# Scores of the first 256 tokens: plain float32 products instead of split ones, with the split of their keys done later

## The chip, the cores and the metric

The kernel runs on one core of a Trainium2 chip. The metric is the device time of one execution in microseconds; the figure given for a kernel is the median of several executions. TensorE (PE) multiplies, VectorE (DVE) and ScalarE (ACT) do elementwise work, GpSimd (POOL) and SyncE (SP) here mostly set up constants and issue transfers.

## The reference

A block-causal attention, a square-relu MLP and a top-1 mixture of experts, in float32:

```python
B, H, S, D = 4, 8, 576, 64
scores = (1/sqrt(D)) * q @ k.T          # block-causal mask, blocks of 64
scores = where(block_i >= block_j, scores, -1e9)
attn = softmax(scores, denominator + 1e-9) @ v
x = attn as [B*S, H*D]                  # 2304 x 512
x = relu(x @ w_in)**2 @ w_out           # 512 -> 2048 -> 512
e = argmax(x @ w_gate + bias[modality]) # 8 experts, 512 -> 1024 -> 512
out = gate * relu(x @ w1[e]) @ w2[e]
```

## The kernel before, in words

The attention is cut into units: for each batch five groups of query rows (`CHUNKS`: four of 128 rows and one of 64), and in each group four pairs of heads. One unit is `attn_pair`, which calls `attn_scores` (scores, softmax, transposes) and `attn_values` (the product with v, and the copy into the x block that the MLP reads). The MLP works on nine blocks of 256 tokens; block j is a list of 16 units and a last step, and `interleave` (L845) puts the attention units that later blocks need between the MLP units of a block. The first eight attention units (batch 0, query groups 1 and 2, so tokens 0 to 255) have nothing to stand beside; they come before the first MLP block. The order on each engine is then made by a planner (`schedule_with_timeline_sim`, L1004) from its own estimates; an instruction traced inside `tc.issue_after(x)` stays behind x on x's engine.

Products that need float32 accuracy are made in one of two ways. Either both operands are split into a high part (a cast to fp32r) and a low part (a subtract), and fp32r products of the parts are added; or both are plain f32. The first MLP block uses plain f32 (`ffn_units32`, L537), all others and the attention use split operands. The inputs q and k are stored twice along the 128 partitions (64 head dimensions each). `split_k` (L225) casts a key tile on ACT (L234) and overwrites the lower 64 partitions with the low part on DVE (L235); `attn_scores` (L281) scales the queries by 0.125 while it casts them on ACT (L300) and gets the low part on DVE (L301). Two fp32r products (L312, L313) per head then give the scores, `both` (L304) handles the two heads of a unit at once: mask, maximum (L315), exp (L317), sum, reciprocal (L320), normalise (L272), transposes (L327), copy (L264).

For batch 0 the keys come in two parts: the first 256 columns (`kpre2`, tiles kw[0] and kw[1]) and the other 320 (`kpre`, kw[2] to kw[4]). Before, part 0 is split just ahead of each of the first four units, part 1 ahead of the four units of query group 3, there inside `issue_after` of the last x copy (L412) of the first eight units. The kw tiles, early v, early q and the MLP's raw weights share one ring of 33 slots, tag `w` (L139), and raw weights are joined from their 64-bit form by `join_weight64` (L150: one ACT and three DVE steps, L156 to L161). PSUM has one bank for the MLP's hidden product (`BANKS`, L46: "h" 1) and two for scores.

Of the kernel before, what the change touches and what calls it, by code (L numbers as in the profile page):

```python
# [20 lines left out]
P = 128  # L21
# [31 lines left out]
def tile_attention_mlp_moe(ctx: ExitStack, tc: tile.TileContext, qT2, kT2, v, w_in, w_out,  # L53
# [168 lines left out]
        kraw[b, h] = apool.tile([P, S], F32, tag="p", bufs=6, name="kraw")  # L222
        nc.sync.dma_start(kraw[b, h], kT2[b, h])

    def split_k(b, hp, part=None):  # L225

        heads = (2 * hp, 2 * hp + 1)
        if part != 1:
            ks2 = apool.tile([P, 2, S], F32R, tag="ks", bufs=4, name=f"ks{b}_{hp}")
            for j, h in enumerate(heads):  # L230
                kst[b, h] = ks2[:, j]

        def split(ks, raw):
            nc.scalar.copy(ks, raw)  # L234
            nc.vector.tensor_sub(ks[HD:P], raw[HD:P], ks[HD:P].bitcast(F32))  # L235

        if part == 0:
            split(ks2[:, :, 0:KS], kpre2[hp])
        else:
            for h in heads:  # L240
                if part is None:
                    split(kst[b, h], kraw[b, h])
                else:
                    split(kst[b, h][:, KS:S], kpre[h])

    def load_v(b, hp, nk):
        vt = apool.tile([P, 5, P], F32, tag="v", bufs=2, name="v")
# [33 lines left out]
    def attn_scores(b, r0, nr, hp, pt2=None):  # L281

        nk = r0 + nr
        nkb = (nk + P - 1) // P
        if (b, r0) in qst:
            qraw = qst[b, r0][:, 2 * hp:2 * hp + 2]
        else:
            qraw = apool.tile([P, 2, P], F32, tag="qraw", bufs=2, name="qraw")
            nc.sync.dma_start(qraw[:, :, :nr], qT2[b, 2 * hp:2 * hp + 2, :, r0:r0 + nr].rearrange("h d s -> d h s"))
        vt = vpre[hp] if b == 0 and nk <= 512 else load_v(b, hp, nk)  # L290
        qlo = apool.tile([P, 2 * P], F32R, tag="qlo", bufs=2, name="qlo")
        qhi = apool.tile([P, 2 * P], F32R, tag="qhi", bufs=2, name="qhi")
        if nr == P:
            dh, dl = (z.rearrange("p (j c) -> p j c", j=2) for z in (qhi, qlo))
        else:

            dh, dl = (z.rearrange("p (j c) -> p j c", j=4)[:, 0::3] for z in (qhi, qlo))
            for z in (qhi, qlo):
                nc.gpsimd.memset(z[:, HD:3 * HD].bitcast(F32), 0.0)
        nc.scalar.mul(dh, qraw[:, :, :nr], 0.125)  # L300
        nc.vector.scalar_tensor_tensor(out=dl, in0=qraw[:, :, :nr], scalar=0.125, in1=dh.bitcast(F32),  # L301
                                       op0=ALU.mult, op1=ALU.subtract)

        def both():  # L304

            nmx = apool.tile([P, 3], F32, tag="nmx", bufs=4, name="nmx")
            sm = apool.tile([P, 4], F32, tag="sm", bufs=4, name="sm")
            pb = apool.tile([P, S], F32, tag="p", bufs=6, name="p")[:, 0:512].rearrange("p (j c) -> p j c", j=2)
            sb = pbank("s", 2).rearrange("p (j c) -> p j c", j=2)
            for j in range(2):  # L310
                ks = kst[b, 2 * hp + j]
                nc.tensor.matmul(sb[:, j], qhi[:, j * P:(j + 1) * P], ks[:, 0:256], start=True, stop=False)  # L312
                nc.tensor.matmul(sb[:, j], qlo[:, j * P:(j + 1) * P], ks[:, 0:256], start=False, stop=True)  # L313
            nc.vector.memset(sb[0:64, :, nk - 64:nk], NEG)
            nc.vector.tensor_reduce(out=nmx[:, 0:2], in_=sb[:, :, :nk], axis=AX.X, op=ALU.max, negate=True)  # L315
            for j in range(2):
                nc.scalar.activation(out=pb[:, j, :nk], in_=sb[:, j, :nk], func=AF.Exp, bias=nmx[:, j:j + 1],  # L317
                                     accum_out=sm[:, j:j + 1])
            nc.vector.tensor_scalar_add(sm[:, 0:2], sm[:, 0:2], 1e-9)
            nc.vector.reciprocal(sm[:, 2:4], sm[:, 0:2])  # L320
            for j in range(2):
                normalise(pb[:, j, :nk], sm[:, 2 + j:3 + j])
            pt = apool.tile([P, 5, P], F32, tag="pt", bufs=2, name="pt")
            tv = pbank("pt", 1).rearrange("p (k q) -> p k q", q=P)
            for i in range(2 * nkb):
                kb = i % nkb
                nc.tensor.transpose(tv[:, i], pb[:, i // nkb, kb * P:(kb + 1) * P], ident)  # L327
            evac_copy(pt[:, 0:2 * nkb], tv[:, 0:2 * nkb])
            return [pt, pt[:, nkb:2 * nkb]]

        def finish_rows(pb, nmx, sm, banks, parts, pt=None):

            npt = len(parts)
            for i, (c0, nv) in enumerate(parts):
                nc.vector.tensor_reduce(out=nmx[:, i:i + 1], in_=banks[i][:, :nv], axis=AX.X, op=ALU.max,  # L335
                                        negate=True)
            if npt == 2:
                nc.vector.tensor_tensor(nmx[:, 0:1], nmx[:, 0:1], nmx[:, 1:2], op=ALU.min)
            for i, (c0, nv) in enumerate(parts):
                nc.scalar.activation(out=pb[:, c0:c0 + nv], in_=banks[i][:, :nv], func=AF.Exp,  # L340
                                     bias=nmx[:, 0:1], accum_out=sm[:, i:i + 1])
            if npt == 2:
                nc.vector.scalar_tensor_tensor(out=sm[:, 0:1], in0=sm[:, 0:1], scalar=1e-9, in1=sm[:, 1:2],
                                               op0=ALU.add, op1=ALU.add)
            else:
                nc.vector.tensor_scalar_add(sm[:, 0:1], sm[:, 0:1], 1e-9)
            nc.vector.reciprocal(sm[:, 2:3], sm[:, 0:1])
            normalise(pb[:, :nk], sm[:, 2:3])
            if pt is None:
                pt = apool.tile([P, 5, P], F32, tag="pt", bufs=2, name="pt")  # L350
            for g0 in range(0, nkb, 4):
                kbs = list(range(g0, min(g0 + 4, nkb)))
                tv = pbank("pt", 1).rearrange("p (k q) -> p k q", q=P)
                for kb in kbs:
                    k0 = min(kb * P, nk - P)
                    nc.tensor.transpose(tv[:, kb - g0], pb[:, k0:k0 + P], ident)
                evac_copy(pt[:, kbs[0]:kbs[-1] + 1], tv[:, 0:len(kbs)])
            return pt

        def single(j):  # L360
            ks = kst[b, 2 * hp + j]
            nmx = apool.tile([P, 3], F32, tag="nmx", bufs=4, name="nmx")
            sm = apool.tile([P, 3], F32, tag="sm", bufs=4, name="sm")
            pb = apool.tile([P, S], F32, tag="p", bufs=6, name="p")[:, 0:512]
            sb = pbank("s", 2)
            nc.tensor.matmul(sb[:, :nk], qhi[:, j * P:(j + 1) * P], ks[:, :nk], start=True, stop=False)
            nc.tensor.matmul(sb[:, :nk], qlo[:, j * P:(j + 1) * P], ks[:, :nk], start=False, stop=True)
            nc.vector.memset(sb[0:64, nk - 64:nk], NEG)
            return finish_rows(pb, nmx, sm, [sb], [(0, nk)], None if pt2 is None else pt2[:, 4 * j:4 * j + nkb])

        def tail():

            half = nk // 2
            nmx = apool.tile([P, 3], F32, tag="nmx", bufs=4, name="nmx")
            sm = apool.tile([P, 3], F32, tag="sm", bufs=4, name="sm")
            pb = apool.tile([P, S], F32, tag="p", bufs=6, name="p")
            banks = []
            for c0 in (0, half):
                sb = pbank("s", 2)
                for j in range(2):  # L380
                    ks = kst[b, 2 * hp + j]
                    for z in (qhi, qlo):
                        nc.tensor.matmul(sb[:, :half], z[:, j * P:(j + 1) * P], ks[:, c0:c0 + half],
                                         start=(j == 0 and z is qhi), stop=(j == 1 and z is qlo))
                banks.append(sb)
            pt = finish_rows(pb, nmx, sm, banks, [(0, half), (half, half)])
            return [pt[:, :, 0:HD], pt[:, :, HD:P]]

        pts = tail() if nr < P else both() if nk <= 256 else [single(j) for j in range(2)]
        return pts, vt  # L390

    def attn_values(b, r0, nr, hp, pairs):
# [45 lines left out]
    def attn_units():  # L438

        res = []  # L440
        for b in range(B):
            for ci, (r0, nr) in enumerate(CHUNKS):
                for hp in range(H // 2):
                    def f(b=b, ci=ci, r0=r0, nr=nr, hp=hp):
                        if b == 0 and ci == 0:
                            split_k(b, hp, 0)
                        elif b == 0 and ci == 2:
                            with tc.issue_after(x_end[0].ins):
                                split_k(b, hp, 1)
                        elif b and ci == 0:  # L450
                            split_k(b, hp)
                        attn_pair(b, r0, nr, hp)
# [555 lines left out]
```

## Time and profile before

| | us |
|---|---|
| median of 3 executions | 878.53 |
| lowest and highest | 877.90, 879.07 |
| the profiled execution, whole | 882.9 |
| its span, first to last instruction | 881.1 |

PE is busy for 97% of the span, PE's weight loads for 83%, DVE for 57%, ACT for 45%, POOL for 8%. The first of 40 slices of the span has PE at 5 tenths, the second at 7, then 9 or more nearly throughout; the DMA engines are full in the first two slices (311 and 353 GB/s). In the profile an engine's rows carry the line of the kernel, the operation and the tiles (written tile, arrow, read tiles). Matmul rows overlap, since the ends of pipelined matmuls are modelled; a plain f32 product of PE appears as two rows with a weight load each.

### The profile page before, as it was taken

The numbers are of one execution on the slowest core, as the hardware profiler recorded it, in microseconds if no ns is written. First come the engines' busy times: TensorE is split into PE (matmuls) and PEld (weight loads), VectorE is DVE, ScalarE is ACT, GpSimd is POOL, SyncE is SP. The second block draws the span as 40 slices with busy tenths as digits, with TensorE's granted clock in tenths as the row PEclk, the third lists the DMA queues.
The fourth block names the chain that finished last, engine by engine and source line by source line (L and its number), as shares of the span: only waits on it lengthen the run. The fifth ranks groups of instructions, "written<-read, shape, count | busy, mean of one in ns | idle before, by whom it ended". The sixth has DMA issues, their size and how long they took to land. (4 is left out here: it accounts for less than half of the span.)

```text
span 881.1 us, 16022 instructions
## 1 busy us (share of the span) xinstructions
PE 851.0 (97%) x5865; PEld 732.1 (83%) x5866; DVE 504.8 (57%) x1533; ACT 399.7 (45%) x1074; POOL 73.4 (8%) x174
## 2 busy tenths in 40 slices
PE   5799999999999999989999999899999999999997
PEld 4566778888988888878888888798889988888896
DVE  6989878978577656554945764427465222222121
ACT  6688888755465434443624443324332211111121
POOL 1000000001000000100000100100203212111011
PEclk9899999999999999999999999999999999999999
DMA  9983151221341220232210211142432111110000
GB/s 311 353 279 119 40 178 41 60 80 28 87 140 60 55 58 31 61 106 77 63 43 32 57 34 52 28 143 73 151 114 58 62 40 54 36 38 34 25 17 37
DMA packets 87922, 73.94 MB, mean 84 GB/s; under 512 B 14305, under 2 KB 75745, under 8 KB 87842
## 3 DMA queue, kind: packets, MB, share of 16 engines
q1 hardware_dynamic: 84194, 63.18, 24.2%
q0 software_dynamic: 3648, 9.72, 3.4%
q8 instruction: 47, 0.77, 0.3%
q14 instruction: 33, 0.27, 0.1%
HBM read 62.71 MB, written 10.42 MB: 83 GB/s over the span
## 5 line engine op out<-in xcount | busy, mean ns | idle before, releaser
L493 PE MATMUL h<-xh,w 128*128 128x256 f32 x512 | 149.9, 293 | 4.6 <-ACT r L506 4.6
L483 PE MATMUL acc<-w,gh 128*128 128x512 f32 x368 | 149.6, 407 | 0.4 <-ACT gh L508 0.4
L495 PE MATMUL h<-xh,w 128*128 128x256 f32 x512 | 146.0, 285 | 0.0
L494 PE MATMUL h<-xl,w 128*128 128x256 f32 x512 | 145.7, 285 | 0.0
L484 PE MATMUL acc<-w,gh 128*128 128x512 f32 x368 | 145.7, 396 | 0.0
L485 PE MATMUL acc<-w,gl 128*128 128x512 f32 x368 | 131.2, 400 | 0.0
L493 PEld LDWEIGHTS h<-xh,w 128*128 128x128 f32 x512 | 97.8, 191 | 10.6 <-ACT r L506 5.9
L506 ACT ACTIVATE r<-h 128x256 f32<-128x256 f32 x128 | 49.3, 385 | 124.5 <-PE h L495 121.1
L507 DVE TENSOR_TENSOR r<-r 128x256 f32<-128x256 f32 x128 | 54.0, 422 | 84.9 <-ACT r L506 84.2
L494 PEld LDWEIGHTS h<-xl,w 128*128 128x128 f32 x512 | 98.0, 191 | 2.8 <-issue 0.2
L495 PEld LDWEIGHTS h<-xh,w 128*128 128x128 f32 x512 | 98.1, 192 | 0.4 <-issue 0.2
L512 DVE SCALAR_TENSOR_TENSOR gl<-pt,gh 128x352 fp32r<-128x352 f32 (+1 forms) x56 | 27.0, 481 | 114.1 <-ACT gh L511 112.7
L511 ACT ACTIVATE gh<-pt 128x352 fp32r<-128x352 f32 (+1 forms) x56 | 24.1, 431 | 134.7 <-PE pt L495 134.7
L485 PEld LDWEIGHTS acc<-w,gl 128*128 128x128 f32 x368 | 67.3, 188 | 15.6 <-issue 1.9
L483 PEld LDWEIGHTS acc<-w,gh 128*128 128x128 f32 x368 | 70.0, 190 | 10.0 <-issue 1.3
L493 PE MATMUL pt<-gxh,w 128*128 128x256 f32 (+1 forms) x256 | 78.1, 305 | 0.0
L495 PE MATMUL pt<-gxh,w 128*128 128x256 f32 (+1 forms) x256 | 77.7, 304 | 0.0
L494 PE MATMUL pt<-gxl,w 128*128 128x256 f32 (+1 forms) x256 | 77.2, 302 | 0.0
L484 PEld LDWEIGHTS acc<-w,gh 128*128 128x128 f32 x368 | 70.1, 190 | 8.3
L508 ACT CAST gh<-r 128x256 fp32r<-128x256 f32 x128 | 52.0, 406 | 47.6 <-DVE r L507 47.6
L509 DVE TENSOR_TENSOR gl<-r,gh 128x256 fp32r<-128x256 f32 x128 | 53.7, 419 | 25.9 <-ACT gh L508 23.1
L340 ACT ACTIVATE p<-s,nmx 128x384 f32<-128x384 f32 (+2 forms) x96 | 56.3, 589 | 22.1 <-DVE nmx L335 13.3
(188 smaller groups left out, 1619.9 us busy)
## 6 DMA issues: line engine op xcount, KB each, us to landing
w<-w_in SPq DMA_DIRECT2D x16, 512.0 KB
w<-w_out SPq DMA_DIRECT2D x16, 512.0 KB
wraw<-w SPq DMA_DIRECT2D x32, 256.0 KB
v<-v SPq DMA_DIRECT2D x28, 256.0 KB
kraw<-kT SPq DMA_DIRECT2D x24, 288.0 KB
qraw<-qT SPq DMA_DIRECT2D x48, 128.0 KB
x2d<-x SPq DMA_DIRECT2D x18, 256.0 KB
v<-v SPq DMA_DIRECT2D x12, 192.0 KB
```

The lines of the kernel that those rows point to most:

```text
L340: nc.scalar.activation(out=pb[:, c0:c0 + nv], in_=banks[i][:, :nv], func=AF.Exp, bias=nmx[:, 0:1], accum_out=sm[:, i:i + 1])
L483: nc.tensor.matmul(acc[t][:n], gh[:, sl], wh, start=(f == 0), stop=False)
L484: nc.tensor.matmul(acc[t][:n], gh[:, sl], wl, start=False, stop=False)
L485: return nc.tensor.matmul(acc[t][:n], gl[:, sl], wh, start=False, stop=(f == nf - 1))
L493: nc.tensor.matmul(hb[:, :bt], whk[:, k, :], xh[:, k, :], start=(k == 0), stop=False)
L494: nc.tensor.matmul(hb[:, :bt], whk[:, k, :], xl[:, k, :], start=False, stop=False)
L495: pe = nc.tensor.matmul(hb[:, :bt], wlk[:, k, :], xh[:, k, :], start=False, stop=(k == KC - 1))
L506: nc.scalar.activation(out=r, in_=hb[:, :bt], func=AF.Relu)
L507: nc.vector.tensor_mul(r, r, r)
L508: act = nc.scalar.copy(gh, r)
L509: dve = nc.vector.tensor_sub(gl, r, gh.bitcast(F32))
L512: dve = nc.vector.scalar_tensor_tensor(out=gl, in0=hb[:, :bt], scalar=0.0, in1=gh.bitcast(F32), op0=ALU.max, op1=ALU.subtract)
```

## The change

For batch 0 and query groups 1 and 2 (`plain`), the queries and keys are no longer split: the new function `first` makes one f32 product per head from the raw tiles. Because both operands are stored twice along the partitions, that product is twice the score, and with the missing factor 0.125 the scale is 0.0625: it is applied to the maximum by a DVE multiplication of a 128x2 tile, and to the scores by the exp's own scale. The part of `both` behind the products becomes `softmax2`, shared by the two. The first 256 key columns of batch 0 are still needed, split, by query groups 3 to 5; their split moves from the first four units to the four units of query group 3, ahead of the split of the other columns, and so inside `issue_after` of the last x copy.

```diff
-    def split_k(b, hp, part=None):
+    def split_k(b, hp):
...
-        if part == 0:
+        if b == 0:
             split(ks2[:, :, 0:KS], kpre2[hp])
-        else:
-            for h in heads:
-                if part is None:
-                    split(kst[b, h], kraw[b, h])
-                else:
-                    split(kst[b, h][:, KS:S], kpre[h])
+        for h in heads:
+            if b:
+                split(kst[b, h], kraw[b, h])
+            else:
+                split(kst[b, h][:, KS:S], kpre[h])
...
+        plain = b == 0 and nk <= 256
+        if not plain:
+            qlo = apool.tile([P, 2 * P], F32R, tag="qlo", bufs=2, name="qlo")
...
+            nc.scalar.mul(dh, qraw[:, :, :nr], 0.125)
+            nc.vector.scalar_tensor_tensor(out=dl, in0=qraw[:, :, :nr], scalar=0.125, in1=dh.bitcast(F32),
+                                           op0=ALU.mult, op1=ALU.subtract)
...
+        def first():
+
+            sb = pbank("s", 2).rearrange("p (j c) -> p j c", j=2)
+            for j in range(2):
+                nc.tensor.matmul(sb[:, j, :nk], qraw[:, j], kpre2[hp][:, j, :nk], start=True, stop=True)
+            return softmax2(sb, 0.0625)
+
+        def softmax2(sb, scale):
...
+            nc.vector.memset(sb[0:64, :, nk - 64:nk], NEG / scale)
             nc.vector.tensor_reduce(out=nmx[:, 0:2], in_=sb[:, :, :nk], axis=AX.X, op=ALU.max, negate=True)
+            if scale != 1.0:
+                nc.vector.tensor_scalar_mul(nmx[:, 0:2], nmx[:, 0:2], scale)
...
-                        if b == 0 and ci == 0:
-                            split_k(b, hp, 0)
-                        elif b == 0 and ci == 2:
+                        if b == 0 and ci == 2:
                             with tc.issue_after(x_end[0].ins):
-                                split_k(b, hp, 1)
+                                split_k(b, hp)
```

## Rows read from the trace of the kernel before

**Rows 1.** The page's first part: busy us (share of the span) xinstructions.

```profile
PE 851.0 (97%) x5865; PEld 732.1 (83%) x5866; DVE 504.8 (57%) x1533; ACT 399.7 (45%) x1074; POOL 73.4 (8%) x174
```

**Rows 2.** Stretches: length, busy us of PE, PEld, DVE, ACT, POOL, PEclk, DMA share, GB/s.

```profile
3.90:8.00 4.10, 1.47 (x4) 1.00 (x4) 1.86 (x4) 2.31 (x5) 0.00 (x0) 1.00 1.13 326
24.00:28.00 4.00, 3.42 (x24) 3.10 (x25) 4.00 (x14) 2.69 (x5) 0.65 (x2) 0.59 1.14 323
40.00:60.00 20.00, 20.00 (x97) 13.60 (x96) 16.50 (x46) 15.03 (x40) 2.03 (x5) 1.00 0.87 290
80.00:100.00 20.00, 20.00 (x116) 14.53 (x115) 19.60 (x53) 18.31 (x44) 1.37 (x6) 1.00 0.15 45
```

**Rows 3.** Groups of 0 to 32 us: count | busy, mean ns | idle before, releasers.

```profile
L312 PE MATMUL s<-ks,qhi 128*128 128x256 f32 x16 | 7.2, 455 | 8.7 <-ACT qhi L300 6.2 <-ACT p L317 1.8 <-DVE ks L235 0.7
...
L300 ACT ACTIVATE qhi<-w 128x256 fp32r<-128x256 f32 x10 | 3.9, 414 | 2.0 <-DMA w<-qT 1.2 <-PE s L312 0.8
L301 DVE SCALAR_TENSOR_TENSOR qlo<-w,qhi 128x256 fp32r<-128x256 f32 x9 | 3.7, 419 | 0.9 <-ACT qhi L300 0.9
...
L235 DVE TENSOR_TENSOR ks<-w,ks 64x512 fp32r<-64x512 f32 x4 | 2.7, 685 | 2.4 <-ACT ks L234 2.3
L234 ACT CAST ks<-w 128x512 fp32r<-128x512 f32 x4 | 2.5, 618 | 3.1 <-DMA w<-kT 3.1
...
L315 DVE TENSOR_REDUCE nmx<-s 128x2 f32<-128x256 f32 x4 | 1.7, 418 | 0.0
...
L320 DVE RECIPROCAL sm<-sm 128x2 f32<-128x2 f32 x8 | 1.1, 149 | 0.0
```

**Rows 4.** The first 32 us in order of time: start, duration, instruction.

```profile
5.74 0.72 ACT L300 ACTIVATE qhi<-w 128x256 fp32r<-128x256 f32 x2 [1.19 <-DMA w<-qT]
...
9.30 0.62 ACT L234 CAST ks<-w 128x512 fp32r<-128x512 f32 x1 [0.58 <-DMA w<-kT]
9.82 0.36 ACT L317 ACTIVATE p<-s,nmx 128x128 f32<-128x128 f32 x1
...
14.82 0.37 ACT L317 ACTIVATE p<-s,nmx 128x128 f32<-128x128 f32 x1
...
22.90 0.47 ACT L317 ACTIVATE p<-s,nmx 128x256 f32<-128x256 f32 x1 [0.16 <-DVE nmx L315]
...
25.75 1.14 DVE L272 TENSOR_SCALAR p<-p,sm 128x256 f32<-128x256 f32 x4
...
31.42 0.37 ACT L412 COPY xf<-pv 128x256 f32<-128x256 f32 x1
```

**Rows 5.** Two stretches at the clock's lower level, columns as in rows 2.

```profile
25.00:26.00 1.00, 1.00 (x13) 1.00 (x10) 1.00 (x5) 1.00 (x2) 0.00 (x0) 0.50 1.11 343
35.00:36.00 1.00, 1.00 (x4) 0.84 (x3) 0.97 (x3) 0.40 (x1) 0.00 (x0) 0.50 1.04 376
```

**Rows 6.** Order of time from 31.68 us, where the third query group starts.

```profile
31.68 2.99 ACT L234 CAST ks<-w 128x320 fp32r<-128x320 f32 x8
...
34.55 0.39 ACT L555 ACTIVATE r<-h 128x256 f32<-128x256 f32 x1
...
34.63 0.44 PE L366 MATMUL s<-ks,qhi 128*128 128x384 f32 x1 [1.66 <-DVE ks L235]
...
35.16 3.50 PE L553 MATMUL h<-xf,w 128*128 128x256 f32 x8
...
38.70 0.38 ACT L555 ACTIVATE r<-h 128x256 f32<-128x256 f32 x1 [3.30 <-PE h L553]
...
39.56 0.47 DVE L235 TENSOR_TENSOR ks<-w,ks 64x320 fp32r<-64x320 f32 x1
```

**Rows 7.** Order of time behind 45 us: a weight join, an MLP unit, a load.

```profile
45.14 0.67 DVE L161 SCALAR_TENSOR_TENSOR w<-w,wf 128x512 int32<-128x512 int32 x1
...
48.80 1.89 PE L553 MATMUL h<-xf,w 128*128 128x256 f32 x8
...
51.99 0.39 SPq L147 DMA_DIRECT2D w<-w_in  x1
```

More of the change, by code (lines that the diff above doesn't have):

```diff
@@ L223, in load_k @@
         nc.sync.dma_start(kraw[b, h], kT2[b, h])
-    def split_k(b, hp, part=None):
+    def split_k(b, hp):
         heads = (2 * hp, 2 * hp + 1)
[L228 to L231, printed above, removed]
+        ks2 = apool.tile([P, 2, S], F32R, tag="ks", bufs=4, name=f"ks{b}_{hp}")
+        for j, h in enumerate(heads):
+            kst[b, h] = ks2[:, j]
         def split(ks, raw):
@@ L290, in attn_scores @@
         vt = vpre[hp] if b == 0 and nk <= 512 else load_v(b, hp, nk)
[L291 to L302, printed above, removed]
+        plain = b == 0 and nk <= 256
+        if not plain:
+            qlo = apool.tile([P, 2 * P], F32R, tag="qlo", bufs=2, name="qlo")
+            qhi = apool.tile([P, 2 * P], F32R, tag="qhi", bufs=2, name="qhi")
+            if nr == P:
+                dh, dl = (z.rearrange("p (j c) -> p j c", j=2) for z in (qhi, qlo))
+            else:
+                dh, dl = (z.rearrange("p (j c) -> p j c", j=4)[:, 0::3] for z in (qhi, qlo))
+                for z in (qhi, qlo):
+                    nc.gpsimd.memset(z[:, HD:3 * HD].bitcast(F32), 0.0)
+            nc.scalar.mul(dh, qraw[:, :, :nr], 0.125)
+            nc.vector.scalar_tensor_tensor(out=dl, in0=qraw[:, :, :nr], scalar=0.125, in1=dh.bitcast(F32),
+                                           op0=ALU.mult, op1=ALU.subtract)
         def both():
-            nmx = apool.tile([P, 3], F32, tag="nmx", bufs=4, name="nmx")
-            sm = apool.tile([P, 4], F32, tag="sm", bufs=4, name="sm")
-            pb = apool.tile([P, S], F32, tag="p", bufs=6, name="p")[:, 0:512].rearrange("p (j c) -> p j c", j=2)
             sb = pbank("s", 2).rearrange("p (j c) -> p j c", j=2)
@@ L313, in both @@
                 nc.tensor.matmul(sb[:, j], qlo[:, j * P:(j + 1) * P], ks[:, 0:256], start=False, stop=True)
-            nc.vector.memset(sb[0:64, :, nk - 64:nk], NEG)
+            return softmax2(sb, 1.0)
+        def first():
[4 more added lines that the diff above has]
+        def softmax2(sb, scale):
+            nmx = apool.tile([P, 3], F32, tag="nmx", bufs=4, name="nmx")
+            sm = apool.tile([P, 4], F32, tag="sm", bufs=4, name="sm")
+            pb = apool.tile([P, S], F32, tag="p", bufs=6, name="p")[:, 0:512].rearrange("p (j c) -> p j c", j=2)
+            nc.vector.memset(sb[0:64, :, nk - 64:nk], NEG / scale)
             nc.vector.tensor_reduce(out=nmx[:, 0:2], in_=sb[:, :, :nk], axis=AX.X, op=ALU.max, negate=True)
+            if scale != 1.0:
+                nc.vector.tensor_scalar_mul(nmx[:, 0:2], nmx[:, 0:2], scale)
             for j in range(2):
-                nc.scalar.activation(out=pb[:, j, :nk], in_=sb[:, j, :nk], func=AF.Exp, bias=nmx[:, j:j + 1],
+                nc.scalar.activation(out=pb[:, j, :nk], in_=sb[:, j, :nk], func=AF.Exp, bias=nmx[:, j:j + 1], scale=scale,
                                      accum_out=sm[:, j:j + 1])
@@ L387, in tail @@
             return [pt[:, :, 0:HD], pt[:, :, HD:P]]
-        pts = tail() if nr < P else both() if nk <= 256 else [single(j) for j in range(2)]
+        pts = first() if plain else tail() if nr < P else both() if nk <= 256 else [single(j) for j in range(2)]
         return pts, vt
```

## The prediction

> **What bounds the kernel now.** I began with the busy shares [rows 1]: PE 97%, the others 57% or less. An average over stages hides what matters here, because the change touches only the first 40 us of 881. So I read the busy times in stretches next [rows 2]. From 40 us on PE has no pause (20.00 of 20 us), while in 3.9 to 8 us it has 1.47 of 4.1. What the kernel can gain at its start is therefore how early PE reaches that gapless stretch, and a microsecond won there stays won only if nothing behind makes PE wait for it again.
>
> Then the groups of instructions of 0 to 32 us [rows 3] and the order of time [rows 4]. Of the first 8 units (two query groups of 128 rows, four head pairs each) the time of each exp is the best milestone: pair 1 at 9.82 us, pair 4 at 14.82, pair 8 at 22.90. The second group so runs at (22.90-14.82)/4 = 2.0 us a pair. The last copy into the x block of the MLP starts at 31.42, 8.5 us after the exp of pair 8; between lies DVE, full without a gap from 24 to 28 us [rows 2], with the joining of the MLP weights put between the steps of pairs 7 and 8: the normalising starts only at 25.75 [rows 4]. TensorE's clock was granted at 0.50, the 1.2 GHz level, at 25 us after PE had waited, and again at 35 us [rows 5]. Its first rows are at that level too, although the column reads 1.00 before the first recorded event: a 128x256 product of fp32r takes 0.455 us by its mean [rows 3], and the first f32 products at 0.50 and later at 1.00 differ as much [rows 6, 7].
>
> Third the place to which the work moves [rows 6]: after the copy at 31.42 ACT makes eight casts of the keys in 2.99 us, and only then (34.55) the relu of the first MLP unit. The `h` bank is single, so unit 2 of the MLP starts on PE at 35.16, right behind that relu; the scores of the third query group wait until 34.63 for DVE's subtract of the keys.
>
> **The change part by part.** All durations are means of [rows 3] unless another group is named.
>
> *Removed from the first 8 units.* On ACT four casts of 128x512 (4 x 0.618 = 2.47 us) and eight scalings of queries (8 x 0.414 = 3.31): 5.8 us. On DVE four subtracts of keys (4 x 0.685 = 2.74) and eight of queries (8 x 0.419 = 3.35): 6.1 us. DVE is the busier engine there, and full before the group ends (4.00 of 4 us [rows 2]), so most of it is on the path.
>
> *Added.* Eight multiplications of a 128x2 tile by 0.0625 on DVE, between the maximum and the exp. No row of before shows it. The nearest are the reciprocal of the same shape (0.149) and the maximum ahead of it over 128x256 (0.418): 1.2 to 3.3 us in all; I take 1.3, by the row of the same shape. It is a dependent step, so each exp comes that much later in its own chain.
>
> *Scores on PE.* Per head one product in f32 takes the place of two in fp32r. Such an f32 product shows as two records: eight records, four 128x256 products, took 1.89 us at the high level [rows 7] and 3.50 at the low one [rows 6], so 0.47 and 0.88 us each. In the first group it has 128 columns, half of that: 0.88 us a pair at the low level where four overlapping products of up to 0.455 stood before, and as many columns pass (2 heads x 4 passes x 128 against 4 x 256): no loss. In the second group it has 256: 0.95 (high) to 1.75 us (low) a pair, half of it new: 0.5 to 0.9 us more a pair, 1.9 to 3.5 in all. PE had pauses there, DVE did not, so I charge a part of it.
>
> The Trainium skill (FP8 and Floating Point Precision, TensorE Precision Notes) says that true FP32 takes four passes of the array. That speaks against the change, which trades two fp32r products for one of these: were PE the bound in the first 20 us, it would give 880.4 (+1.9). The trace agrees on the price, by the 3.50 and 1.89 us, but not that PE is the bound there.
>
> *The path to the last copy.* Pair 1 needs only its queries (landed at 5.74) and no split: product 0.88, then mask, maximum (0.418) and multiplication, some 1.1 us with the hand-over, so its exp starts at about 7.7 instead of 9.82. Pair 4 cannot go before its keys, at 9.30 [rows 4]: exp at 11.3 if PE is free, 12.0 if not, instead of 14.82: 3 us won. In the second group DVE loses 0.42 us a pair and gets 0.16 back, PE grows to some 2.1 us a pair at the high level, as long as the present 2.0; the first pair may still be at the low level (+0.9). Exp of pair 8: 3 - 0.4 - 0.8, about 1.8 us won. In the tail, where DVE has no gap, its queue is shorter by what was removed, less the multiplications (6.1 - 1.3 = 4.8), of which 1.8 is already counted; of the other 3.0 I take 2.2, because the joins of further weights may fill some of it. The last copy is 4.0 us earlier. Bounds: 1.0 (PE at the low level through the second group: 3.5 us more PE work set against 3.0 won, and a little of the tail) and 6.0 (all that DVE and ACT lose).
>
> *Moved to the third group.* The four wide casts (2.47 us) now stand on ACT behind that copy, for the block that holds them back orders them so, and the four subtracts (2.74) on DVE. Queued behind them: on ACT the first relu, and through the single `h` bank MLP unit 2 on PE; on DVE the subtract that the third group's first scores wait for. At least the first pair's wide subtract is in that chain (+0.69). At most all four casts stand ahead of the relu (+2.47). ACT stands idle for 3.3 us behind that relu now, until 38.70 [rows 6], so the later pairs' casts can go there: I take 1.2.
>
> *What is free.* The first keys stay in their two slots of the `w` ring until the third group instead of until about 10 us. Behind them is SP's queue: the weight loads that reuse a slot. Those are issued at 51.99 us [rows 7], when the third group's splits have long ended (40.03), so 10 us cover it; were they gone, the two loads would come later by what is missing. No DMA is added, moved or passed. The masking value and the exp's scale cost no instruction.
>
> *Sum.* -4.0 + 1.2 = -2.8 us at the start of the gapless stretch. Whether it stays: the joins for MLP unit 5 end at 45.8 (w_in) and its products start at 48.80 [rows 7], 3 us of slack, and DVE has net 3.35 - 1.3, about 2 us less to do by then. So the lead fits, with 0 to 1.5 us to be given back later; I take 0. The profiled execution took 882.9 us (span 881.1, 1.8 around it), 0.5% above the median of 878.53; -2.8 makes it 880.1, and on the median 875.7. Bounds: -6.0 + 0.7 = -5.3, and -1.0 + 2.5 + 1.5 = +3.0.
>
> **The rivals.**
> (a) *DVE is the bound behind 40 us and gives most back.* DVE has 19.60 of 20 us at 80 to 100 us [rows 2], so PE cannot run ahead of it; then only DVE's balance counts: 3.35 removed for good, 1.3 added, -2.05, of which the pauses that remain in the first 20 us take some: -1.5. That gives 877.0. Against it: PE has not one pause in that stretch. The Trainium skill (Perfetto Trace Analysis, Identifying the Most-Contended Engine) would have PE judged by its weight loads, not by its matmuls: by that PE is at 13.60 of 20 us at 40 to 60 us and DVE with 16.50 is the fuller. Here a plain f32 product streams longer than its weights load (PE full, PEld 68%), so the rule understates PE; the trace bears it out only in part.
> (b) *Slower: the moved casts hold the first relu.* The four wide casts all stand before the relu on ACT, +2.47 us from the last copy to MLP unit 2, and the first pair's split adds 0.7 on DVE. It decides where the copy comes less than 2.5 us earlier, which is so if PE stays at the low level through the second group (copy 1.0 earlier): +1.5 to +2.2, 880.3. For it: eight casts stand before the relu today. Against it: the casts of pairs 3 and 4 aren't needed before the relu, and the 3.3 us of idle ACT behind it are room for them.
> (c) *The clock does not fall.* PE is denser in the first 20 us and waits less. Unit 2 of the MLP pays 3.50 - 1.89 = 1.6 us for the lower level, the stretch at 25 us up to as much again [rows 5 to 7]; without both another 2.9 us is won: 872.8. For it: both fell after waits that get shorter. Against it: the wait for the third group's keys gets longer.
> (d) *The change does nothing that can be seen.* The order on the engines is made by the planner from its own times, and it may fill the freed time with joins that are not urgent, so that the copy comes when it did: 878.5.
>
> **How the numbers follow.** Forecast 875.7 (own range 874.3 to 877.0): 0.44. (a) 0.23, (b) 0.15, (c) 0.12, (d) 0.06. Leaving out 0.2: from 872.5 to 880.5. A measurement of this kernel can tell about 0.2%, 1.76 us, from no change, so faster means below 876.8. Faster: 0.41 of the forecast, 0.12 of (c) and 0.04 of (a), 0.57. Slower: 0.14 of (b), 0.01 of (d), 0.15. Same: the rest, 0.28.
>
> **What would show it.** In the changed profile: the first exp near 7.7 us and the fifth near 14; no cast of keys before the last x copy, and that copy at 27 to 28 us; twelve casts behind it, with the first relu 3 to 4 us after it; PE gapless from about 36 us; the gated stretch at 25 us shorter or gone. The prediction is wrong if the first copies come earlier but MLP unit 3 still starts near 40.6 us (then (a), (b) or (d)), or if the second group's products hold PE at the low level.

## The result, and the profile after

| | before | after |
|---|---|---|
| median, us | 878.43 | 887.95 |
| lowest and highest | 877.90, 879.07 | 883.30, 891.08 |
| executions | 4 | 4 |
| profiled execution, span | 881.1 | 884.9 |

The changed kernel takes 1.0105 times as long, 95% interval 1.0072 to 1.0138: 9.5 us slower, where 2.8 us faster was forecast. Measured again beside other kernels it took 884.73 us against 877.7, 1.0075 (1.0051 to 1.0099); the loss is so some 7 to 9 us. The profiled execution of before shown ahead of the prediction is one of its longer ones; below, `before_again` is a second one, with a span of 877.6 us.

The busy shares after, as in [rows 1], say little: PE has the same busy time and nearly the same share.

```profile
PE 851.2 (96%) x5865; PEld 731.0 (83%) x5866; DVE 506.3 (57%) x1533; ACT 396.9 (45%) x1066; POOL 73.0 (8%) x174
```

The start after, in order of time (start, duration, instruction), which answers to [rows 4]:

```profile
5.82 1.19 PE L317 MATMUL s<-w 128*128 128x128 f32 x4 [5.82 <-DMA w<-qT]
...
7.77 0.17 DVE L327 TENSOR_SCALAR nmx<-nmx 128x2 f32<-128x2 f32 x1
8.02 1.28 ACT L329 ACT_TABLE_LOAD   x1 [7.89 <-DVE nmx L327]
...
9.32 0.37 ACT L329 ACTIVATE p<-s,nmx 128x128 f32<-128x128 f32 x1
...
13.50 1.18 PE L317 MATMUL s<-w 128*128 128x256 f32 x4 [0.40 <-ACT p L329]
13.75 0.37 ACT L329 ACTIVATE p<-s,nmx 128x128 f32<-128x128 f32 x1
...
21.06 0.70 DVE L158 SCALAR_TENSOR_TENSOR wf<-w,wf 128x512 int32<-128x512 int32 x1
...
21.84 0.67 DVE L158 SCALAR_TENSOR_TENSOR wf<-w,wf 128x512 int32<-128x512 int32 x1
...
22.49 0.68 DVE L161 SCALAR_TENSOR_TENSOR w<-w,wf 128x512 int32<-128x512 int32 x1
...
23.10 0.68 DVE L325 TENSOR_REDUCE nmx<-s 128x2 f32<-128x512 f32 x1
...
24.55 0.47 ACT L329 ACTIVATE p<-s,nmx 128x256 f32<-128x256 f32 x1 [0.73 <-DVE nmx L327]
```

Two things stand in the way here. A load of the activation table stands at 8.02 us in front of the first exp, on the path; in before it ran in the shadow of the first transfers, ahead of the first cast:

```profile
0.85 1.28 ACT L234 ACT_TABLE_LOAD   x1 [0.71 <-PEq L1000]
```

And DVE does more steps of weight joins ahead of the maximum of pair 8 than it did: five, the last three (L158 to L161) from 21.06 to 23.17. In before there were three, the last of them this one, and the maximum followed at 22.19:

```profile
21.59 0.67 DVE L158 SCALAR_TENSOR_TENSOR wf<-w,wf 128x512 int32<-128x512 int32 x1
```

What follows the last x copy, which answers to [rows 6]:

```profile
29.96 0.35 ACT L424 COPY xf<-pv 128x256 f32<-128x256 f32 x1
30.21 0.62 ACT L233 CAST ks<-w 128x512 fp32r<-128x512 f32 x1
...
31.31 4.16 ACT L233 CAST ks<-w 128x320 fp32r<-128x320 f32 x10
...
34.60 0.69 PE L378 MATMUL s<-ks,qhi 128*128 128x384 f32 x1 [2.47 <-DVE ks L234]
...
35.95 0.44 ACT L233 CAST ks<-w 128x320 fp32r<-128x320 f32 x1
36.30 0.37 ACT L565 ACTIVATE r<-h 128x256 f32<-128x256 f32 x1
36.72 3.78 PE L563 MATMUL h<-xf,w 128*128 128x256 f32 x8 [0.47 <-ACT r L565]
...
42.34 1.03 PE L563 MATMUL h<-xf,w 128*128 128x256 f32 x4
```

All twelve casts, wide and narrow, stand between the copy and the first relu, with two join steps among them: the relu comes 6.3 us behind the copy instead of 3.1, and MLP unit 2 waits for it. Unit 3 starts at 42.34, before at 40.56. DVE is full meanwhile. TensorE had 1.72 us of work in the 4 us up to 30; its granted clock fell between 30 and 31 us and was 0.50 (1.2 GHz) from then to 40 us (columns as in [rows 2]; the stretches overlap):

```profile
26.00:30.00 4.00, 1.72 (x20) 1.27 (x20) 3.99 (x10) 3.47 (x9) 0.00 (x0) 1.00 1.21 307
28.00:32.00 4.00, 2.73 (x20) 1.79 (x20) 4.00 (x9) 3.47 (x9) 0.00 (x0) 0.84 1.11 339
32.00:36.00 4.00, 1.53 (x5) 1.14 (x4) 3.84 (x8) 4.00 (x11) 0.00 (x0) 0.50 1.11 339
36.00:40.00 4.00, 3.53 (x9) 2.65 (x9) 3.93 (x9) 1.28 (x5) 0.00 (x0) 0.50 1.04 373
```

So 1.8 us are lost at the start; the loss is several times that. The order of the instructions on each engine tells where to look next: it differs between the two kernels up to some 340 us (2199 of PE's 5865 rows, a little over half of ACT's and DVE's) and is the same behind that, though the diff touches nothing past 42 us. The planner laid out that stretch anew, and in it PE has waits that `before_again` does not have, or has shorter (timeline of after):

```profile
129.36 0.53 PE L493 MATMUL acc<-w,gh 128*128 128x512 f32 x1 [1.98 <-ACT gh L518]
...
300.23 1.09 PE L414 MATMUL pv<-pt,v 128*64 128x128 f32 x16 [1.75 <-DMA v<-v]
306.36 1.09 PE L414 MATMUL pv<-pt,v 128*64 128x128 f32 x16 [0.83 <-DVE sm L358]
```

In `before_again` the first of these products waits 0.47 us and the values near 300 us none:

```profile
127.12 0.50 PE L483 MATMUL acc<-w,gh 128*128 128x512 f32 x1 [0.47 <-ACT gh L508]
...
300.10 1.09 PE L402 MATMUL pv<-pt,v 128*64 128x128 f32 x16
```

### The profile page after: what moved, and what is told of

Its sections match the earlier page's. It is cut to its first block, busy times and chain, and to the rows that moved or that the text cites. A ratio compares the mean times of both kernels' runs of the same rounds, so it can differ in the third digit from the quotient of the medians.

```text
span 884.9 us, 16006 instructions
## 1 busy us (share of the span) xinstructions
PE 851.2 (96%) x5865; PEld 731.0 (83%) x5866; DVE 506.3 (57%) x1533; ACT 396.9 (45%) x1066; POOL 73.0 (8%) x174
```

## The experiments

Theory A: the loss is made in the first 42 us (late first exp, moved casts ahead of the relu). Theory B: it is made behind, by the planner's new order. In the first set before took 877.7 us (26 executions).

**The changed kernel again** (`after_again`), no edit.

> The changed kernel once more, unaltered, for its own spread and a second profile. Theory A (the loss is in the first 42 us: the first exp comes late, the moved casts hold the first relu): the start is alike in both profiles (first exp 9.3 us, third MLP unit at 42.3), and the rest of the span repeats, so the times lie within 1 us of each other. Theory B (what costs most is behind 42 us, in an order that the planner has changed for the first third of the program, and it falls out differently from run to run): the start is alike but the times spread again over 883 to 891 us, and the profiles differ in where PE waits after 42 us.

884.73 us, 1.0075 (1.0051 to 1.0099), from 881.16 to 886.67: a wider spread than A said, a lower one than B did. Copy at 29.50, relu at 35.87, unit 3 at 42.04 us; the waits for gh and v are there again with 1.62 and 1.64 us.

**The table loaded early** (`early_table`).

```diff
+    warm = const.tile([P, 1], F32, name="warm")
+    nc.scalar.activation(out=warm, in_=w8[:, 0:1], func=AF.Exp)
```

> The changed kernel with one tiny exp of a constant ahead of everything on ACT. The order of all other instructions on every engine is that of the changed kernel. In the profile of the changed kernel ACT's table load (1.28 us) stands at 8.02 us, behind the maximum of the first unit, and the first exp starts at 9.32; before it stood at 0.85. Theory A: the load goes to 1.5 to 3 us, the first exp starts at 8.0 to 8.1, the last x copy comes up to 1.3 us earlier, and the kernel is 0.5 to 1.5 us faster than the changed one. Theory B: the start gains the same, but the time stays inside the changed kernel's spread (883 to 891).

883.37 us, 1.0071 (1.0049 to 1.0093): no gain that can be told. The load is at 0.84 and the first exp at 7.95 us; the fourth is 1.1 us earlier than in after, the fifth only 0.15, because the product between them now runs at TensorE's lower level (by its duration; the clock's column reads 1.00 throughout the first 20 us). The timeline of this kernel, to be set beside 13.50 and 13.75 above (the fifth exp of after is at 16.63):

```profile
7.95 0.37 ACT L331 ACTIVATE p<-s,nmx 128x128 f32<-128x128 f32 x1 [5.61 <-DVE nmx L329]
...
12.38 2.07 PE L319 MATMUL s<-w 128*128 128x256 f32 x4 [0.42 <-ACT p L331]
12.63 0.37 ACT L331 ACTIVATE p<-s,nmx 128x128 f32<-128x128 f32 x1
...
16.48 0.48 ACT L331 ACTIVATE p<-s,nmx 128x256 f32<-128x256 f32 x1
```

The same four records take 2.07 us where after took 1.18. Copy and unit 3 come at 30.21 and 42.59, no earlier than in after. The table is a true cost at its place and worth nothing at the end of the stretch.

**Plain scores alone** (`scores_only`): the split stays with the first four units.

```diff
+                        if b == 0 and ci == 0:
+                            split_k(b, hp, 0)
+                        elif b == 0 and ci == 2:
...
-                                split_k(b, hp)
+                                split_k(b, hp, 1)
```

> One part of the change alone: plain f32 scores in the first eight units, but the split of the first 256 key columns stays ahead of the first four units, as before (so the first ACT instruction is a cast again and the table load is early). Theory A: first exp at 8 to 8.5 us, only eight casts behind the last x copy, first relu within 3.3 us of it, third MLP unit at 39 to 40.5 us instead of 42.3; time 2 to 3.5 us below the changed kernel. Theory B: the start gains that, but the time stays near 885 or above, because the order from 42 to 250 us is nearly that of the changed kernel.

883.77 us, 1.007 (1.0048 to 1.0092). With eight casts behind the copy (31.82) unit 3 starts at 39.51, a microsecond before that of before, and still the kernel is slower. Its order is that of after from 113 us on, with waits of 1.17 us for gh at 127.50 and 1.31 for v at 297.77. A alone can't be the whole. (The profiled execution, 880.25 us, is the fastest of the eight.)

**The split behind the relu** (`relu_first`): for pairs 2 to 4 it is held behind the first relu.

```diff
-                            with tc.issue_after(x_end[0].ins):
+                            with tc.issue_after((r_end if hp and r_end else x_end)[0].ins):
...
-            nc.scalar.activation(out=r, in_=hb[:, :BT], func=AF.Relu)
+            r_end.append(nc.scalar.activation(out=r, in_=hb[:, :BT], func=AF.Relu))
```

> The changed kernel, except that the key splits of head pairs 2 to 4 are held behind the first relu of the MLP on ACT instead of behind the last x copy (the first pair's stay where they are). Theory A: relu about 2.5 us earlier than 36.3, second MLP unit at 33.5 to 34.5 instead of 36.7, third at 39.5 to 40.5 instead of 42.3; 1.5 to 3 us faster than the changed kernel. Rival C (the casts do not hold the relu, the second unit waits for the scores of the third query group, which need DVE): unit 2 still starts behind 36 us and nothing is won.

882.61 us, 1.0044 (1.002 to 1.0068), 2.1 us under `after_again`. The copy is at 31.47, the relu at 34.16, unit 3 at 40.41: the loss at the start is gone, so it was the casts that held the relu. Unit 2 comes right behind it, and at the higher clock (1.00 from 24 to 44 us; below, with the same unit of `after_again` and of `before_again`):

```profile
34.57 1.99 PE L564 MATMUL h<-xf,w 128*128 128x256 f32 x8 [1.54 <-ACT r L566]
```

```profile
36.33 3.78 PE L563 MATMUL h<-xf,w 128*128 128x256 f32 x8
```

```profile
37.01 1.99 PE L553 MATMUL h<-xf,w 128*128 128x256 f32 x8
```

The intervals of this kernel and of `after_again` overlap, so the gain in time is less sure than that at the relu. More than half of the loss in time is left.

The next set forces orders (before: 878.59 us, 31 executions). Behind the first eight units the instructions of PE, ACT, DVE and SP are chained in a given order, by edges that add no semaphore, and the planner has no choice there. No run forces a kernel's own order on it, so what the edges cost by themselves is known only from `scores_old_order` (1.0002): nothing, unless the plain scores win as much.

```diff
+            if prev is not None and engine in ('PE', 'Activation', 'DVE', 'SP'):
+                tc.add_manual_dep(have[at], prev.name, nosync, reason="order")
+            prev = have[at]
```

**Before beside itself** (`before_again`), no edit.

> The kernel before, unaltered, for a second profile: the first one was taken of an execution of 882.9 us, 4 to 5 us above its median. Theory B (the order behind 42 us): an execution near 878 us, with PE waits of at most 1 us in all between 100 and 145 us and none between 285 and 320 us, as in the first profile, and without that one's low clock near 390 and 570 us. If instead waits of 1.5 us or more stand in those two stretches, they are no mark of the new order and theory B loses its places.

878.41 us, 1.0000 (0.9971 to 1.0029).

**Before's work in the new order** (`before_new_order`).

> The kernel before with none of the change's edits, but with everything behind the first eight units queued on PE, ACT, DVE and SP in the order that the planner chose for the changed kernel (edges of issue order alone, no waits). Theory B: 3.5 to 6 us slower than before (881 to 884), with the PE waits of the changed kernel at 125 to 130 us (relu's cast, 1.5 to 2 us) and near 297 us (v's transfer, 1 to 2 us). Theory A (the loss is at the start): within 1 us of before.

880.94 us, 1.0026 (1.0007 to 1.0045). Not one instruction of the change is in it, and it is slower, by 2.3 us where B said 3.5 to 6. The unit at 297 us waits for v (timeline), and the products behind that wait are at the lower clock (a stretch, columns as in [rows 2]):

```profile
297.16 1.92 PE L456 MATMUL pv<-pt,v 128*64 128x128 f32 x16 [2.02 <-DMA v<-v]
```

```profile
298.00:300.00 2.00, 2.00 (x15) 1.67 (x12) 0.26 (x1) 0.96 (x2) 0.07 (x1) 0.50 0.42 35
```

**After's work in the old order** (`after_old_order`), the moved splits left free.

> The changed kernel with all its edits, but with everything behind the first eight units, except the moved splits, queued in the order of the kernel before. Theory B: the two stretches with new PE waits are gone, and only the start remains (third MLP unit 1 to 3 us later than before's 40.6, since four wide casts now stand ahead of the others): 878.5 to 881, 4 to 6 us faster than the changed kernel. Theory A: as slow as the changed kernel, 883 to 887, or slower.

884.22 us, 1.0045 (1.002 to 1.007), slower than B said (878.5 to 881). The waits behind are as in `before_again` (0.63 us for gh, none for v near 300), and the loss that shows is at the start: unit 3 at 45.92. Here the third group's scores are late, because DVE has all four wide subtracts (the first at 33.62) ahead of the first narrow one (timeline):

```profile
36.34 0.69 DVE L288 TENSOR_TENSOR ks<-w,ks 64x512 fp32r<-64x512 f32 x1
37.78 1.29 DVE L288 TENSOR_TENSOR ks<-w,ks 64x512 fp32r<-64x512 f32 x2
...
39.56 0.49 DVE L288 TENSOR_TENSOR ks<-w,ks 64x320 fp32r<-64x320 f32 x1
40.11 0.69 PE L434 MATMUL s<-ks,qhi 128*128 128x384 f32 x1 [6.53 <-DVE ks L288]
```

**Plain scores alone in the old order** (`scores_old_order`).

> Plain scores alone, the split left in the first four units, and everything behind the first eight units in the order of the kernel before. Theory B: what the plain scores win at the start (third MLP unit at 39 to 39.5 us instead of 40.6) is all that is left: 876 to 878, 0.5 to 2 us faster than before and 5 to 7 us faster than the same kernel in the planner's new order (883.8). Theory A: 883 or above, as the run in the new order.

878.52 us, 1.0002 (0.9979 to 1.0025): the plain scores as such cost or gain nothing that can be told. Unit 3 came at 43.12, not at 39 to 39.5.

The last set asks for the place of the order's cost and for the price of the split's place (before: 876.91 us, 23 executions).

**Two mixed orders** (`before_mixed_order`, `after_mixed_order`): the new order up to about 245 us, the old one from there.

> The work of the kernel before. Behind the first 8 units its instructions are forced into the order of the changed kernel up to about 245 us, and into their own old order from there on. Theory B, made narrower: what the planner's new order costs is lost between the third and the fourth block of the MLP, where the values of an attention unit wait for their v (2.02 us near 297 us with the new order throughout, none with the old). Then the time between the third and the fourth store of x2 goes back from 71.0 to about 65.7 us, and the kernel takes 878.4 us, as before, or down to 876 if the 2.7 us that the new order is ahead at the third store are a real lead. The rival is that the loss is made in the first 245 us, by the waits for gh near 126 and 136 us: then it stays at 880.9.

> The work of the changed kernel, in the same mixed order: its own up to about 245 us (but for the moved splits, which are left free), that of the kernel before from there on. If theory B holds with its place (values that wait for v near 300 us), some 2.5 us come back: 882 against 884.7. If the whole of the loss is made in the first 42 us (theory A), the changed order costs nothing that matters, and it takes 884 to 885.

881.72 us, 1.0047 (1.0029 to 1.0066), and 885.49 us, 1.0099 (1.0068 to 1.013): both expectations failed. The stretch between the third and the fourth store of x2 did go back to 65.7 us (before: 65.7 in `before_again`, 71.05 in `before_new_order`). But the stretch ahead of it grew from 75.6 to 82.4 us (81.6 with after's work). At the seam stands a wait of its own, followed by the lower clock (`before_mixed_order`, timeline, then a stretch):

```profile
254.63 1.99 PE L456 MATMUL pv<-pt,v 128*64 128x64 f32 x40 [3.16 <-DMA v<-v]
```

```profile
256.00:258.00 2.00, 1.09 (x14) 0.91 (x12) 1.40 (x5) 2.00 (x7) 0.00 (x0) 0.50 0.94 341
```

And the stretches do not hold the same work in different orders. Up to the third store, and from there to the fourth, `before_again` (first two lines) has 1752 and 489 instructions of PE, `before_new_order` (the next two) 1740 and 504. From the second store to the third `before_again` has 605 and `before_mixed_order` 628 (the last two lines, in this order):

```profile
0.00:270.50 270.50, 251.82 (x1752) 202.98 (x1753) 218.00 (x655) 189.65 (x521) 15.03 (x74) 0.99 0.46 141
270.50:336.21 65.71, 65.68 (x489) 57.21 (x490) 40.44 (x143) 31.04 (x92) 2.04 (x2) 1.00 0.19 54
```

```profile
0.00:267.77 267.77, 249.74 (x1740) 201.54 (x1742) 216.47 (x647) 188.47 (x517) 14.97 (x74) 0.99 0.46 141
267.77:338.82 71.05, 69.03 (x504) 59.80 (x503) 44.22 (x151) 32.60 (x95) 2.10 (x2) 0.98 0.21 54
```

```profile
194.90:270.50 75.60, 73.08 (x605) 64.17 (x604) 52.76 (x175) 39.03 (x112) 4.25 (x14) 1.00 0.32 89
```

```profile
192.32:274.70 82.38, 78.01 (x628) 68.58 (x626) 54.91 (x179) 41.06 (x115) 4.25 (x14) 0.96 0.31 84
```

The 2.7 us that the new order is ahead at the third store (267.77 against 270.50) are so not all a lead: it has done less by then. The wait at 297 us belongs to the order behind 245 us, but these two kernels can't tell what the rest of the new order costs: the mixture is a third order, with work of its own at the seam.

**Wide splits late, old order** (`wide_late_old_order`): as `after_old_order`, but the wide splits of pairs 2 to 4 stand behind the first relu.

```diff
+            else:
+                with tc.issue_after(x_end[0].ins):
+                    narrow()
+                with tc.issue_after(r_end[0].ins):
+                    split(ks2[:, :, 0:KS], kpre2[hp])
```

> The work of the changed kernel in the order of the kernel before, as in after_old_order, but the wide splits of head pairs 2 to 4 are held back behind the first relu of the MLP; the narrow splits and the first pair's wide one stay where they were. Theory A, made narrower: what the moved split costs is that the wide subtractions of pairs 2 to 4 (3 x 0.69 us on DVE) and their casts stand ahead of the narrow subtraction that the third group's first scores wait for, so that these start at 40.11 us and MLP unit 3 at 45.92. Then the scores come at about 37.5 to 38, unit 3 at about 43.5, and the time falls from 884.2 to about 881.5. If it is not where they stand but their work as such that costs (DVE has less room for the joins of the weights), unit 3 may start earlier but the time stays near 884.

879.57 us, 1.003 (1.0016 to 1.0043). Scores at 35.58 instead of 40.11, the relu 4.2 us behind the copy, unit 3 at 42.12 instead of 45.92 (timeline):

```profile
34.00 0.41 ACT L636 ACTIVATE r<-h 128x256 f32<-128x256 f32 x1
34.27 1.68 ACT L287 CAST ks<-w 128x512 fp32r<-128x512 f32 x3
35.03 0.49 DVE L288 TENSOR_TENSOR ks<-w,ks 64x320 fp32r<-64x320 f32 x1
35.58 0.69 PE L445 MATMUL s<-ks,qhi 128*128 128x384 f32 x1 [3.29 <-DVE ks L288]
...
36.38 3.62 PE L634 MATMUL h<-xf,w 128*128 128x256 f32 x8
```

By the ratios the time falls by 0.15%, and the two intervals overlap; the earlier start is shown, its worth in time only points that way.

**The same with the early table** (`wide_late_table_old_order`).

> As wide_late_old_order, and the table of the exponential is loaded at the start, by an exp of one column ahead of everything else on ACT. The 1.28 us of the load leave the path of the first exp. If that path sets the start of MLP unit 3, unit 3 comes 1.3 us earlier and the kernel takes about 880, and with every cost of the changed kernel that has been found taken out, 878 or less. If DVE and its joins set it, the load costs nothing: the same time as wide_late_old_order, within 0.2%.

879.01 us, 1.0017 (1.0001 to 1.0033). Unit 3 starts at 43.38, not 1.3 us earlier: the table is not what sets it. With every cost that was found taken out, the change is where before is, or just above; no version beats it.

## Why the prediction was wrong

**The first exps.** The product at 5.82 and the multiplication at 7.77 came within 0.3 us of what was worked out (the exp at 7.95 where no load is in its way, `early_table`), but the exp was at 9.32 instead of 7.7: my sum took the casts off ACT and did not see that the first of them also carried the table load, 1.28 us, hidden until then. The fourth pair's exp came at 13.75 (forecast 11.3 to 12), and with the load out of the way at 12.63. The multiplications were sized right: eight took 1.3 us.

**The pace of the second group.** Forecast 2.3 us a pair (2.0, and 1.2 us of the lead of 3 given back over four pairs), measured (24.55 - 13.75)/4 = 2.7, so that pair 8 was 1.65 us later than before and not 1.8 earlier. The f32 products ran at the higher level there (1.03 to 1.18 us a pair); pair 7 was still 0.5 us ahead (20.72 against 21.22), and between it and pair 8 came the joins on DVE from 21.06 to 23.17. This is what rival (d) named: the planner fills the freed time with joins.

**The last copy.** The tail shrank from 8.5 to 5.4 us, more than the 2.2 I took, so the copy was 1.5 us earlier (31.42 to 29.96) in the first pair of traces and 4.0 (33.46 to 29.50) in the second. The two kernels before differ by 2.0 us there, as keys landed later in `before_again` (second cast of keys at 8.30 against 6.94). The term of 4.0 lies at the edge of what the runs show; its bounds held.

**The moved splits: the term that failed.** I took 1.2 us, because the casts of later pairs would go into ACT's idle time behind the relu. From the copy to the start of unit 2, and on to that of unit 3, it took, in us:

| kernel | copy | to unit 2 | unit 2 took | unit 3 | copy to unit 3 |
|---|---|---|---|---|---|
| before | 31.42 | 3.7 | 3.50 | 40.56 | 9.1 |
| `before_again` | 33.46 | 3.6 | 1.99 | 40.90 | 7.4 |
| `scores_only` | 31.82 | 4.1 | 1.99 | 39.51 | 7.7 |
| after | 29.96 | 6.8 | 3.78 | 42.34 | 12.4 |
| `after_again` | 29.50 | 6.8 | 3.78 | 42.04 | 12.5 |
| `early_table` | 30.21 | 6.8 | 3.78 | 42.59 | 12.4 |
| `relu_first` | 31.47 | 3.1 | 1.99 | 40.41 | 8.9 |

With the split moved, unit 2 starts 3.0 to 3.3 us later behind the copy than in before, not 1.2; even the largest value that I allowed on ACT, 2.47, was too small, because two join steps of 0.67 us stand among the casts. That it goes back to 3.1 when the split of pairs 2 to 4 is held behind the relu shows the cause. The rest is the clock, which the sum left as it was: unit 2 takes 3.78 us at 0.50 in the three traces of the table with twelve casts ahead of the relu, 3.50 at 0.50 in before, and 1.99 at 1.00 in the others. In the first pair of traces the copy's lead of 1.5 us was eaten by the casts alone. In the second the copy was 4.0 us earlier, as forecast, and unit 2 still 0.7 earlier (36.33 against 37.01); the 1.8 us that it took longer at the lower clock made unit 3 1.1 us late.

Rival (b) had the mechanism and, in the first pair, the size (+1.5 to +2.2 us; measured +1.8, in the second pair +1.1) and the condition (a copy less than 2.5 us earlier); in the second pair the condition was not met, and it was the clock, which (b) doesn't have, that made unit 3 late. I gave (b) 0.15, on the ground that the casts of pairs 3 and 4 are not needed before the relu. Not needed does not mean not placed there: `issue_after` bounds a block from one side only, and eight casts stood before the relu already [rows 6]. Its time, 880.3, was too low all the same, as it lacks the order's price (below).

**Whether it stays.** The sum took nothing to be given back behind the start. No lead came, so only delays can be followed, in one and the same order. Starts of the stores of x2 (the output of each block of the MLP), in us behind `before_again` (spans 877.6, 881.1, 878.7, 883.0):

| old order | unit 3 | second store | fourth | last |
|---|---|---|---|---|
| `before_again` | 40.90 | 194.90 | 336.21 | 643.90 |
| before | -0.3 | -2.1 | -2.4 | +3.3 |
| `scores_old_order` | +2.2 | +1.6 | +1.3 | +1.1 |
| `after_old_order` | +5.0 | +4.1 | +3.0 | +4.6 |

The first two rows are one kernel, so 2 to 3 us can come from the execution. The 5 us of `after_old_order` are not swallowed (0.45% in time as well); of the 2.2 us of `scores_old_order` nothing is left in time (1.0002). How much of a small lead would stay is not shown.

**What no step of the sum had.** The planner orders the program anew up to 340 us when its first 40 us change. I had its freedom as rival (d), but only for the first 40 us and at nothing lost. `before_new_order` puts the price of the new order on before's work at 0.26%, some 2.3 us. On `scores_only` the planner's own order costs 0.7%, and 0.02% with the old one forced: about 6 us. So an order's price is not a constant that can be added; what is shown is that order alone costs between 2 and 6 us here. After's loss of 7 us so has two sources: the place of the moved split (2.1 us come back in `relu_first`, and the old order with the split where it fell still loses 0.45%), and the order behind.

A part of the order's price can be placed. In all six traces with a new order throughout, PE waits 1.3 to 2.1 us for v between 297 and 301 us; in the eight with the old order there, the profile shows no wait of PE from 280 to 335 us. From the third store to the fourth `after_again` takes 4.0 us more than `before_again` (69.68 against 65.71): 1.9 us are busy time of PE, for work that stood ahead before (504 instructions against 489), and 2.1 us are waits, 1.64 and 0.51 for v. The rest is open. The wait for gh is longer in five of the six (1.1 to 2.0 us against 0.4 to 0.7 in the old order), and the 6 us of `scores_only` can't be seen in its trace, that of its fastest execution, whose span is that of `scores_old_order` (878.6 and 878.7). Whether room for a third v tile would remove the wait near 300 us was not tried.

**The other rivals.** (a) is not borne out: PE, not DVE, is full behind 40 us (20.00 of 20 us from 40 to 60, DVE 17.90; from 80 to 100, where (a) has it, 20.00 and 16.22). But no lead reached that stretch, so what DVE would have made of one is not shown. (c) held at one place and failed at the other: at 25 us the clock was granted at 1.00, but it fell at 30 us, and unit 2 took 3.78 us against 3.50 [rows 6], where `before_again` shows that before can have it at 1.99.

## What to carry to other kernels

Look at what the instruction that you remove carries with it: the first activation on ACT holds the table load, and behind an operand that comes late it is on the path. Work that is moved behind a point should also be bounded on its other side, by the first thing that must not wait for it (here the relu), and the narrow splits that others wait for should stand ahead of the wide ones. Where a planner orders the program, compare the orders before the durations: force the old order on the new work and the new order on the old work, and the two causes come apart, as far as an order's price is the same for both. Before you compare a stretch in two orders, count the instructions in it.

## What the runs showed of the hardware

The table load waits with the instruction that it stands in front of: with a first activation that depends on data it started at 7.9 to 8.15 us in every kernel without the early exp or the early cast, else at 0.84 or 0.85. The Trainium skill (ScalarE: Activation LUTs, What ACT_TABLE_LOAD costs) gives 1283 ns for the load and about 1380 ns for a drain, for every switch to a different set. The trace agrees on the load (1.28 us). At this load, the only one of the execution, no drain shows: it starts 0.08 us behind the multiplication that it waits for, and the exp at 9.32, 0.02 us behind its end.

A wait of PE of 2 us in the middle of the dense stretch was followed by a granted clock of 0.50 in some traces (after 2.02 us at 297 in `before_new_order`, after 2.15 at 397 in `after_again`; after 3.16 at 254 in `before_mixed_order`) and not in others (2.12 us at 255 and 2.24 at 568 in `before_again`, 1.00 throughout the next 4 us), so a wait can cost more than its length, and not in every execution:

```profile
568.02 1.39 PE L402 MATMUL pv<-pt,v 128*64 128x64 f32 x40 [2.24 <-DMA v<-v]
```

```profile
570.00:572.00 2.00, 2.00 (x14) 1.81 (x13) 0.46 (x2) 0.38 (x1) 0.53 (x14) 1.00 0.55 166
```
